# Inverse norms ahead of ELU work on ScalarE, and ELU's maximum moved between ScalarE and VectorE in three steps

## The chip, the cores and the metric

The kernel runs on one core of one Trainium2 chip. The metric is the device time of one execution in microseconds (us), as the median of several executions. The profile of one execution shows a span that is about 1.8 us shorter than that execution's device time, because the time also holds what lies outside the first and last instruction.

## The reference, cut to what matters

A linear attention feeds a two-layer perceptron:

```python
# q, k, v: (8, 8, 576, 64); g_norm: (64,); w_in: (512, 2048); w_out: (2048, 512)
kv = np.einsum('bhsd,bhse->bhde', k, v)
out = np.einsum('bhsd,bhde->bhse', q, kv)
rms = np.sqrt(np.mean(out * out, axis=-1, keepdims=True) + 1e-06)
attn = out / rms * g_norm
x = attn.transpose(0, 2, 1, 3).reshape(8 * 576, 512)
h = x @ w_in
g = np.where(h > 0.0, h, np.exp(np.minimum(h, 0.0)) - 1.0)      # ELU
return g @ w_out
```

The 4608 rows of `x` are worked in nine groups (0 to 8) of 512.

## The kernel before

For each group, TensorE does the first product `mm1` in eight steps (`h_ps`, two PSUM banks a step, 8 matmuls), then the second product `mm2` (`o_ps`). Between them stands ELU: ScalarE takes the exponential from PSUM, and VectorE does `min(e, 1) - 1` and then the maximum with `h`. The maximum reads `h` from PSUM, so it is what frees the two banks. With `relu`, ScalarE copies `relu(h)` out of PSUM first, so ScalarE frees the banks, and VectorE adds from SBUF instead.

```python
def elu(T, i, ps, relu):
    ...
    for lo, hi, h in parts:
        nc.scalar.activation(e[:, lo:hi, :], h, AF.Exp)
    if relu:
        r = mlpt.tile([P, 2, G], BF16, name="elu_h", tag="elu_h", bufs=2)
        for lo, hi, h in parts:
            nc.scalar.activation(r[:, lo:hi, :], h, AF.Relu)
        parts = [(0, 2, r)]

    def rest():
        nc.vector.tensor_scalar(out=e, in0=e, scalar1=1.0, scalar2=1.0, op0=ALU.min, op1=ALU.subtract)
        for lo, hi, h in parts:
            nc.vector.tensor_tensor(
                out=gT[T][:, 2 * i + lo : 2 * i + hi, :], in0=e[:, lo:hi, :], in1=h,
                op=ALU.add if relu else ALU.max)
    return rest
```

While a group's `mm1` runs, the attention of the next group is worked in pieces, for each half `h` of its rows: `se` (TensorE's score product into the PSUM tile `at`, of which there is one, and the square on ScalarE), `sum` (VectorE), `inv` (ScalarE: Ln, then Exp of -0.5 times that), `mul` (VectorE scales `at` into `xs`, which frees `at`, and the DMA engines transpose `xs` into `xT`), and `gain` (VectorE multiplies `xT` by `g_norm`). Group 1 is written out by hand, group 2 uses `window`:

```python
at = attention(2)
rest = {}
for i, tag in enumerate("mBAmBAmB"):        # PSUM banks: m (two single ones), pair A, pair B
    rest[i] = mm1(1, i, tag, i in (4, 5, 7))    # the last argument: relu
    if i == 2: at["kv"]()
    if i == 3: at["se0"]()
    if i == 5:
        at["sum0"](); at["inv0"](); at["mul0"](); rest[4]()
    if i == 6:
        at["se1"](); rest[5]()
    if i < 4: rest[i]()
at["sum1"](); at["inv1"](); rest[6](); at["mul1"](); rest[7]()
...                                         # then group 1's second product, its first tiles in pair A
def window(T, at, early, late, second):
    for i in range(8):
        rest = mm1(T, i, "BA"[i % 2])           # no relu
        for name in early.get(i, ()): at[name]()
        if i in second: second[i]()             # a piece of the second product of group T - 1
        rest()
        for name in late.get(i, ()): at[name]()
# T == 2:
early = {2: ("sum0", "inv0"), 5: ("sum1", "inv1"), 6: ("gain0",), 7: ("gain1",)}
late = {0: ("kv",), 1: ("se0",), 2: ("mul0",), 4: ("se1",), 5: ("mul1", "ahead")}
```

(Some lines are joined here, and "..." marks cuts.) In the traces each engine works through its own instructions in the order in which they are written: in the profile below, a Ln whose input was complete at 59.40 us starts at 61.62, behind two relus and an exponential (58.91 to 61.76) that stand ahead of it in the program.

## Time and profile before

The median is 291.17 us, of 3 executions between 291.03 and 291.43.

The profile's page gives the busy share of each engine and the granted TensorE clock in 40 slices of the span (tenths; 9 is 90% or more):

```profile
PE 276.6 (96%) x2085; PEld 128.8 (45%) x2121; DVE 167.4 (58%) x225; ACT 138.1 (48%) x201; POOL 49.2 (17%) x89
...
PEclk9999999999999999999999999999999999999999
```

TensorE (PE) is busy for 96% of the span at full clock. So the other engines cost time only where TensorE waits for them. The view of waits, for TensorE between 46 and 103 us (engine, its line and what it waited for: us in total, times, longest):

```profile
PE at L250 <- DVE xs L299: 2.1, 1, 2.1
PE h_ps L378 <- DVE xT L312: 0.9, 2, 0.4
PE h_ps L378 <- DVE gT L362: 0.4, 2, 0.2
```

The longest is explained by the timeline (start in us, length in us, engine, line, what is written from what, count; in brackets the idle time before it and what ended it):

```profile
56.05 5.35 PE L378 MATMUL h_ps<-xT,w_in_sb 128*128 128x512 bf16 x24
...
58.18 1.22 DVE L283 TENSOR_REDUCE ss<-sq 128x16 f32<-128x1024 bf16 x1
58.91 1.02 ACT L354 ACTIVATE elu_h<-h_ps 128x1024 bf16<-128x1024 f32 x1
59.81 1.03 ACT L350 ACTIVATE elu_e<-h_ps 128x1024 bf16<-128x1024 f32 x1
60.72 1.04 ACT L354 ACTIVATE elu_h<-h_ps 128x1024 bf16<-128x1024 f32 x1
...
61.62 0.33 ACT L291 ACTIVATE ss<-ss,eps_col 128x16 f32<-128x16 f32 x1
61.98 0.22 ACT L292 ACTIVATE ss<-ss 128x16 f32<-128x16 f32 x1
...
62.23 1.23 DVE L299 TENSOR_TENSOR xs<-at,ss 128x1024 bf16<-128x1024 f32 x1 [2.83 <-ACT ss L292]
...
63.50 0.41 PE L250 MATMUL at<-kv_sb,qT 64*128 64x64 bf16 x16 [2.10 <-DVE xs L299]
...
69.16 1.22 DVE L299 TENSOR_TENSOR xs<-at,ss 128x1024 bf16<-128x1024 f32 x1
...
74.23 0.49 DVE L312 TENSOR_SCALAR xT<-xT,g_col 128x1024 bf16<-128x1024 bf16 x1 [2.39 <-DMA xT<-xs]
...
74.82 1.89 PE L378 MATMUL h_ps<-xT,w_in_sb 128*128 128x512 bf16 x7 [0.44 <-DVE xT L312]
```

VectorE's sums (`ss<-sq`) are complete at 59.40. But the Ln and Exp of those sums stand in ScalarE's queue behind a relu, an exponential and another relu, and end at 62.20. Only then can VectorE scale `at` into `xs` (62.23 to 63.46), and only then can TensorE write its next scores into `at`, at 63.50. TensorE's last 24 matmuls before that start at 56.05. Counted with one 512-column matmul each 0.216 us (the eight from 63.85 to 65.58 us in this profile take 1.73 us), the slot of the last one (the time until the next could start) ends at 61.24. So TensorE stands idle for 2.26 us. The view of waits says 2.10, because it counts from the modelled end of the matmul, 61.40.

The second scale (69.16) leads, over the transposes, to the gain that ends at 74.72, and TensorE starts group 2 at 74.82.

### The profile page before, as it was taken

The page shows a single profiled execution, that of the slowest core. Times are in us where ns is not written, and L with a number is a line of the kernel's source. Part 1 is how long each engine was busy: PE and PEld are TensorE (multiplying, and loading weights), DVE is VectorE, ACT ScalarE, POOL GpSimd, SP SyncE. Part 2 cuts the span into 40 slices and gives each one's busy share as a digit, 9 for nine tenths or more (in the row PEclk, how much of TensorE's full clock was granted, in tenths as well). Part 3 has the DMA queues.
Part 4 walks back from the last instruction along what each step waited for, and adds up shares of the span by engine and source line. Part 5 has one row for each costly group of instructions (what it writes and reads, how often), then busy time and mean ns, then how long its engine had stood idle before and what let it go on. Part 6 is the DMA issues. An engine that isn't in the chain of part 4 may idle for free.

```text
span 288.4 us, 5107 instructions
## 1 busy us (share of the span) xinstructions
PE 276.6 (96%) x2085; PEld 128.8 (45%) x2121; DVE 167.4 (58%) x225; ACT 138.1 (48%) x201; POOL 49.2 (17%) x89
## 2 busy tenths in 40 slices
PE   7899999979999999999999999999999999999994
PEld 3444444434444344444444444444444444444443
DVE  3349732869278647862786377637774776344600
ACT  3578358683365345534554355425552555343311
POOL 7643303323034033003300330000000000000000
PEclk9999999999999999999999999999999999999999
DMA  7999999899799669869935892542140235030222
GB/s 210 184 204 206 206 270 220 182 278 137 119 259 166 136 105 286 107 116 253 222 41 102 227 239 66 93 101 73 36 97 15 73 39 109 0 75 0 73 73 74
DMA packets 50571, 39.46 MB, mean 137 GB/s; under 512 B 30964, under 2 KB 44020, under 8 KB 50548
## 3 DMA queue, kind: packets, MB, share of 16 engines
q0 software_dynamic: 15008, 21.30, 37.0%
q1 hardware_dynamic: 35136, 17.31, 30.4%
q10 hardware_dynamic: 404, 0.53, 0.5%
q8 instruction: 16, 0.26, 0.4%
q14 instruction: 7, 0.06, 0.1%
HBM read 36.70 MB, written 9.44 MB: 160 GB/s over the span
## 4 chain that ended last, share of the span: by engine, by line
PE 85%; DVE 6%; DMA 4%; issue 2%; ACT 2%; SPq 1%; DVEq 0%
PE h_ps L378 38%; PE o_ps L399 37%; DVE gT L362 2%; PE h_ps L566 2%; DMA first_v<-in_v_dram 2%; DMA xT<-xs 2%; PE at L250 2%; PE at L156 1%; PE o_ps L436 1%; DVE elu_e L358 1%; PE kv_ps L156 1%; DVE xs L299 1%; PE mean L199 1%; DVE ss L283 1%; ACT elu_e L350 1%
## 5 line engine op out<-in xcount | busy, mean ns | idle before, releaser
L399 PE MATMUL o_ps<-w_out_sb,gT 128*128 128x512 bf16 x548 | 128.6, 379 | 0.7 <-issue 0.2
L378 PE MATMUL h_ps<-xT,w_in_sb 128*128 128x512 bf16 x530 | 126.5, 379 | 2.3 <-DVE xT L312 0.9
L350 ACT ACTIVATE elu_e<-h_ps 128x1024 bf16<-128x1024 f32 (+1 forms) x79 | 74.1, 954 | 92.1 <-PE h_ps L378 81.2
L362 DVE TENSOR_TENSOR gT<-elu_e,h_ps 128x1024 bf16<-128x1024 bf16 (+1 forms) x73 | 81.1, 1118 | 7.2 <-PE h_ps L378 0.5
L399 PEld LDWEIGHTS <-gT 128*128 128x128 bf16 x560 | 54.4, 98 | 65.8 <-issue 0.9
L378 PEld LDWEIGHTS <-w_in_sb 128*128 128x128 bf16 x552 | 52.3, 98 | 63.2 <-DVE xT L312 0.9
L358 DVE TENSOR_SCALAR elu_e<-elu_e 128x1024 bf16<-128x1024 bf16 x72 | 32.3, 449 | 64.8 <-ACT elu_e L350 64.8
L415 ACT COPY o_sb<-o_ps 128x512 f32<-128x512 f32 x32 | 18.4, 588 | 23.8 <-PE o_ps L399 23.1
L103 POOL CAST q_bf<-st_q 128x384 bf16<-128x384 f32 x36 | 18.1, 546 | 34.3 <-DMA st_q<-in_q_dram 34.3
L283 DVE TENSOR_REDUCE ss<-sq 128x16 f32<-128x1024 bf16 x14 | 17.0, 1218 | 4.9 <-ACT sq L277 4.9
L299 DVE TENSOR_TENSOR xs<-at,ss 128x1024 bf16<-128x1024 f32 x14 | 17.1, 1219 | 2.8 <-ACT ss L292 2.8
L277 ACT ACTIVATE sq<-at 128x1024 bf16<-128x1024 f32 x14 | 14.4, 1026 | 0.8 <-PE at L250 0.8
L339 POOL COPY gate<-qT 1x32 bf16<-1x32 bf16 x5 | 1.0, 199 | 69.1 <-DMA qT<-q_bf 69.1
L212 DVE SCALAR_TENSOR_TENSOR xT<-y_ps,g_col,rT 128x512 bf16<-128x512 f32 (+1 forms) x10 | 6.2, 641 | 11.0 <-ACT rT L209 9.0
L312 DVE TENSOR_SCALAR xT<-xT,g_col 128x1024 bf16<-128x1024 bf16 x14 | 6.7, 481 | 4.5 <-DMA xT<-xs 4.5
L156 PEld LDWEIGHTS <-k_bf 64*64 64x64 bf16 x576 | 6.3, 107 | 5.6 <-issue 5.6
L90 POOL DMA_DIRECT2D k_bf<-in_k_dram x11 | 7.9, 722 | 2.6 <-DMA w_in_sb<-in_moe_w_in_dram 1.8
L90 POOL DMA_DIRECT2D v_bf<-in_v_dram x11 | 7.7, 697 | 4.2 <-DMA w_in_sb<-in_moe_w_in_dram 2.1
L250 PE MATMUL at<-kv_sb,qT 64*128 64x64 bf16 (+1 forms) x248 | 6.1, 192 | 2.1 <-DVE xs L299 2.1
L250 PEld LDWEIGHTS <-qT 64*128 64x128 bf16 (+1 forms) x248 | 4.4, 97 | 8.2 <-issue 8.0
L112 DVE COPY o_sb<-o_ps 128x256 f32<-128x256 f32 x1 | 0.4, 425 | 11.1 <-PE o_ps L436 11.1
L354 ACT ACTIVATE elu_h<-h_ps 128x1024 bf16<-128x1024 f32 x6 | 6.2, 1030 | 0.0
(55 smaller groups left out, 100.8 us busy)
## 6 DMA issues: line engine op xcount, KB each, us to landing
st_q<-in_q_dram POOLq DMA_DIRECT2D x6, 1152.0 KB, 7.0
out_dram<-o_sb SPq DMA_DIRECT2D x24, 256.0 KB, 3.3
k_bf<-in_k_dram POOLq DMA_DIRECT2D x6, 576.0 KB, 9.2
v_bf<-in_v_dram POOLq DMA_DIRECT2D x6, 576.0 KB, 12.3
out_dram<-o_sb SPq DMA_DIRECT2D x19, 128.0 KB, 2.4
w_out_sb<-in_moe_w_out_dram POOLq DMA_DIRECT2D x4, 512.0 KB, 15.0
w_in_sb<-in_moe_w_in_dram POOLq DMA_DIRECT2D x2, 512.0 KB, 11.0
q_bf<-in_q_dram POOLq DMA_DIRECT2D x3, 288.0 KB, 13.4
```

Source lines behind the costliest of these rows:

```text
L90: eng.dma_start(out=dst.rearrange("p m j d -> p m (j d)"), in_=in_[:, ms, :])
L103: nc.gpsimd.tensor_copy(out=bf["q", b][:, u, js], in_=raw[b][:, u::2, js, :].rearrange("p l j d -> p j l d"),)
L250: nc.tensor.matmul(se_ps[lo:hi, l, (4 * i + m) * 64 : (4 * i + m) * 64 + 64], lhsT=qT[b][l * 64 : l * 64 + 64, s, u, j : j + n, :], rhs=kv ...
L277: nc.scalar.activation(sq, st["se", h], AF.Square)
L283: nc.vector.reduce_sum(out=ss, in_=st.pop(("sq", h)).rearrange("p l (m e) -> p (l m) e", e=D), axis=AX.X,)
L299: nc.vector.tensor_tensor(out=st["xs"][:, 2 * h : 2 * h + 2, :].rearrange("p i (l m e) -> p l i m e", l=2, e=D), in0=se_ps.rearrange("p l ...
L350: nc.scalar.activation(e[:, lo:hi, :], h, AF.Exp)
L358: nc.vector.tensor_scalar(out=e, in0=e, scalar1=1.0, scalar2=1.0, op0=ALU.min, op1=ALU.subtract)
L362: nc.vector.tensor_tensor(out=gT[T][:, 2 * i + lo : 2 * i + hi, :], in0=e[:, lo:hi, :], in1=h, op=ALU.add if relu else ALU.max,)
L378: nc.tensor.matmul((ps[a] if isinstance(ps, list) else ps[:, a, :])[:, cols], lhsT=w_in_sb[:, c, f * P : f * P + P], rhs=xT[T][:, c, cols] ...
L399: nc.tensor.matmul(o_ps[T, j], lhsT=gT[T][:, f, j * P : j * P + P], rhs=w_out_sb[:, f, :], start=(f == 0), stop=(f == FC - 1),)
L415: nc.scalar.copy(o_sb[T, half][:, j % 2, :], o_ps[T, j])
```

## The change

The intent is to compute the inverse norms as soon as their sums are there, and to balance ELU's maximum: in group 1's step 5 it goes from ScalarE back to VectorE, and in group 2's steps 3 and 5 from VectorE to ScalarE. The second scale of group 1 (`mul1`) is also written ahead of step 6's work on VectorE. `"later"` returns the relu as a function of its own, so that the inverse norms can be written ahead of it.

```diff
-        if relu:
+        def freed():
             r = mlpt.tile([P, 2, G], BF16, name="elu_h", tag="elu_h", bufs=2)
             for lo, hi, h in parts:
                 nc.scalar.activation(r[:, lo:hi, :], h, AF.Relu)
-            parts = [(0, 2, r)]
+            parts[:] = [(0, 2, r)]
+        if relu and relu != "later":
+            freed()
 ...
-        return rest
+        return (freed, rest) if relu == "later" else rest
 ...
-        rest[i] = mm1(1, i, tag, i in (4, 5, 7))
+        rest[i] = mm1(1, i, tag, "later" if i in (4, 7) else False)
+        if i < 4:
+            rest[i]()
         if i == 2:
             at["kv"]()
         if i == 3:
             at["se0"]()
-        if i == 5:
+        if i == 4:
             at["sum0"]()
             at["inv0"]()
+            freed, rest[4] = rest[4]
+            freed()
+        if i == 5:
             at["mul0"]()
             rest[4]()
+            rest[5]()
         if i == 6:
             at["se1"]()
-            rest[5]()
-        if i < 4:
-            rest[i]()
     at["sum1"]()
     at["inv1"]()
+    at["mul1"]()
+    freed, rest[7] = rest[7]
+    freed()
     rest[6]()
-    at["mul1"]()
     rest[7]()
 ...
-    def window(T, at, early, late, second):
+    def window(T, at, early, late, second, relu=()):
         for i in range(8):
-            rest = mm1(T, i, "BA"[i % 2])
+            rest = mm1(T, i, "BA"[i % 2], i in relu)
 ...
-        window(T, at, early, late, second)
+        window(T, at, early, late, second, (3, 5) if T == 2 else ())
```

## The prediction

> **What bounds it.** TensorE: 276.6 of 288.4 us busy (96%) in the engine table, full clock in every slice, 85% of the chain of waits. VectorE (58%) and ScalarE (48%) matter only where TensorE waits for them. The change touches 48 to 100 us of the timeline. A 512-column matmul starts every 0.216 us; stepped with that, TensorE's gaps there are:
>
> - 61.45 to 63.50: group 2's second score product waits 2.05 us for `xs` (VectorE) to free `at`.
> - 74.2 to 74.82: 0.6 us for group 2's gained `xT`.
> - 88.80 to 88.97 and 94.15 to 94.51: 0.5 us for the maximum that frees pair A in group 2's steps 3 and 5.
> - 99.7 to 100.27: 0.6 us for group 3's gained `xT`.
>
> So at most 3.75 us is to be had.
>
> **Group 1.** The 2.05 us is ScalarE's queue: the sums end at 59.40, but Ln and Exp (0.33 + 0.22 us) stand behind relu 4, exp 5 and relu 5 (1.02 us each) and end at 62.20. Afterwards they follow exp 4 and end near 60.0; `xs` is done near 61.3, before TensorE asks. All 2.05 us goes.
>
> Given back: without step 5's relu, pair A is freed by a VectorE maximum instead of ScalarE (61.76). VectorE runs scale (1.22), step 4 (0.57 + 0.7) and step 5 (0.43 + 1.22) from 60.05: free near 64.3. TensorE wants A near 63.55: a new wait of about 0.75 us. The maximum takes 1.22 us, the add from SBUF 0.69[...].
>
> The second scale ends near 67.3 instead of 70.4. [...] transposes took 6.5 us to land while loads ran (to 68 us), later ones 2.4. So part of those 3 us is lost; I estimate `xT` gained at 72 to 72.5. TensorE finishes its 40 matmuls (8.85 us from 64.35) at 73.2, without a wait. Group 2 starts there instead of at 74.82: **1.6 us saved**.
>
> **Group 2.** Two more 1.02 us ScalarE activations find room (12.8 us busy of 25). They free A about 1.5 us sooner and shorten a VectorE operation from 1.22 to 0.69. The A waits go, but TensorE then waits longer for `xT`; only what the second scale gains counts. Ln starts as before, since the sums end only then. **About 0.4 us saved.**
>
> ScalarE gets one activation more in all.
>
> **Prediction:** 291.17 - 2.0 = 289.2 us, 8 in 10 between 288.4 and 290.2. Faster by over 2%: 0.02; within 2%: 0.97; slower by over 2%: 0.01.
>
> **What would show it.** The TensorE wait for `xs` is gone; Ln of the first norms starts near 59.5; a new TensorE wait for the `gT` maximum, 0.5 to 1 us, precedes group 1's second product, which ends without a wait for `xT`; group 2's waits for `gT` are gone, and one for `xT` remains near its end, as long or longer.
>
> **What would make it wrong.** GpSimd's casts (from 63.2 us) may slow VectorE (its min/subtract took 0.57 and 0.72 us there, not 0.43), so that A comes later. The second transposes may land later behind the loads. In group 2, stores or loads may delay the last transposes (4.1 us from scale to landing) or, begun earlier, let them land sooner.

Its sum is 1.6 + 0.4 = 2.0 us; the operation times, 1.22 and 0.69 us, and the landing times, 6.5 and 2.4 us, are read from the trace.

## More of the kernel before

With each execution comes the mean clock that TensorE was granted, as a share of full speed.

The profiled execution took 290.18 us.

## The result, and the profile after

The changed kernel took 288.5 us in the median, the kernel before 291.1 in the same rounds. The ratio is 0.9905, with a 95% interval of 0.9886 to 0.9925. A ratio here is the mean time of one kernel's fast runs over that of the other's of the same rounds, so it is not quite the ratio of the medians. The saving was 2.6 to 2.8 us where I had said 2.0. The median lies 0.1 us inside my range, and 0.9905 of 291.1 us is 288.3, just below it.

One of the four executions, the profiled one, took 484.63 us at a mean clock of 0.559, and is slow. Its profile says nothing about the change and is not used. I ran the changed kernel again under the label `again`. Its profiled execution took 288.27 us, and what follows is read from it. Line numbers have moved: the maximum or add that writes `gT` was L362 and is L366, min/subtract was L358 and is L362.

The waits of TensorE between 46 and 103 us, changed kernel:

```profile
PE h_ps L382 <- DVE xT L312: 0.9, 1, 0.9
PE o_ps L403 <- DVE gT L366: 0.5, 1, 0.5
```

The timeline of the changed kernel, for the same stretch as above:

```profile
58.47 1.21 DVE L283 TENSOR_REDUCE ss<-sq 128x16 f32<-128x1024 bf16 x1
59.72 0.31 ACT L291 ACTIVATE ss<-ss,eps_col 128x16 f32<-128x16 f32 x1 [0.63 <-DVE ss L283]
60.06 0.22 ACT L292 ACTIVATE ss<-ss 128x16 f32<-128x16 f32 x1
60.18 1.00 ACT L355 ACTIVATE elu_h<-h_ps 128x1024 bf16<-128x1024 f32 x1
60.31 1.23 DVE L299 TENSOR_TENSOR xs<-at,ss 128x1024 bf16<-128x1024 f32 x1 [0.62 <-ACT ss L292]
...
61.59 0.41 PE L250 MATMUL at<-kv_sb,qT 64*128 64x64 bf16 x16
...
63.10 1.22 DVE L366 TENSOR_TENSOR gT<-elu_e,h_ps 128x1024 bf16<-128x1024 bf16 x1
...
64.38 8.79 PE L403 MATMUL o_ps<-w_out_sb,gT 128*128 128x512 bf16 x40 [0.55 <-DVE gT L366]
...
66.08 1.22 DVE L299 TENSOR_TENSOR xs<-at,ss 128x1024 bf16<-128x1024 f32 x1 [0.62 <-ACT ss L292]
...
71.26 0.49 DVE L312 TENSOR_SCALAR xT<-xT,g_col 128x1024 bf16<-128x1024 bf16 x1 [0.42 <-DMA xT<-xs]
...
73.01 1.89 PE L382 MATMUL h_ps<-xT,w_in_sb 128*128 128x512 bf16 x7
```

The wait of 2.1 us for `xs` is gone. Ln starts at 59.72, `xs` is written by 61.54, and TensorE's scores start at 61.59. The slot of the last matmul before them ends at 61.33, so 0.26 us of the gap are left here, and 0.10 us in a second profile of the same kernel (`again_b`, below). In its place stands the new wait that I expected: pair A is now freed by VectorE's maximum (63.10 to 64.32), and TensorE starts the second product at 64.38, 0.72 us after the slot of its last matmul ended (61.93 + 8 x 0.216 = 63.66). The second scale now starts at 66.08 instead of 69.16, its `xT` is gained by 71.75, and group 2 starts at 73.01, without a wait for it.

The profile of the changed kernel spans 286.5 us, that of the kernel before 288.4. That is 1.9 us, almost exactly my 2.0. So the puzzle is not in these two profiles. It is why the timed executions differ by 0.7 us more than the profiled ones.

### The profile page after: what moved, and what is told of

Read it like the earlier page. It is cut to its first block, busy times and chain, and to the rows that moved or that the text cites. A ratio compares the mean times of both kernels' runs of the same rounds, so it can differ in the third digit from the quotient of the medians.

```text
span 482.8 us, 5110 instructions
## 1 busy us (share of the span) xinstructions
PE 470.4 (97%) x2085; PEld 170.3 (35%) x2121; DVE 166.4 (34%) x225; ACT 140.4 (29%) x202; POOL 47.8 (10%) x89
## 4 chain that ended last, share of the span: by engine, by line
PE 97%; issue 2%; DVE 0%; DVEq 0%
PE o_ps L403 44%; PE h_ps L382 43%; PE h_ps L570 2%; PE o_ps L440 1%; PE at L250 1%; PE at L156 1%; PE kv_ps L526 1%; PE qt_ps L174 1%; PE kv_ps L156 1%; PE mean L199 1%; PE mean L526 0%; PE y_ps L189 0%; PE y_ps L526 0%; DVE kv_sb L112 0%; DVE o_sb L112 0%
## 5 line engine op out<-in xcount | busy, mean ns | idle before, releaser
L403 PE MATMUL o_ps<-w_out_sb,gT 128*128 128x512 bf16 x548 | 222.7, 582 | 2.2 <-issue 1.2
L382 PE MATMUL h_ps<-xT,w_in_sb 128*128 128x512 bf16 x530 | 215.5, 579 | 3.9 <-issue 2.4
L403 PEld LDWEIGHTS <-gT 128*128 128x128 bf16 x560 | 72.7, 131 | 139.6 <-issue 137.8
L382 PEld LDWEIGHTS <-w_in_sb 128*128 128x128 bf16 x552 | 70.6, 131 | 128.5 <-issue 125.6
L362 DVE TENSOR_SCALAR elu_e<-elu_e 128x1024 bf16<-128x1024 bf16 x72 | 30.7, 427 | 216.3 <-ACT elu_e L350 216.3
L366 DVE TENSOR_TENSOR gT<-elu_e,h_ps 128x1024 bf16<-128x1024 bf16 (+1 forms) x72 | 79.8, 1116 | 7.4 <-DVE elu_e L362 0.9
L103 POOL CAST q_bf<-st_q 128x384 bf16<-128x384 f32 x36 | 16.8, 509 | 31.8 <-DMA st_q<-in_q_dram 27.6
L156 PEld LDWEIGHTS <-k_bf 64*64 64x64 bf16 x576 | 7.9, 131 | 8.8 <-issue 8.0
L570 PE MATMUL h_ps<-xT,w_in_sb 128*128 128x512 bf16 x24 | 9.8, 579 | 0.0
L112 DVE COPY qT<-qt_ps 128x1024 bf16<-128x1024 bf16 (+1 forms) x8 | 3.3, 453 | 12.6 <-PE qt_ps L174 12.6
```

Source lines behind the costliest of these rows:

```text
L103: nc.gpsimd.tensor_copy(out=bf["q", b][:, u, js], in_=raw[b][:, u::2, js, :].rearrange("p l j d -> p j l d"),)
L156: nc.tensor.matmul(kv_ps[s][l * 64 : l * 64 + 64, u * 64 : u * 64 + 64], lhsT=bf["k", b][rows, 2 * l + u, j, :], rhs=bf["v", b][rows, 2 * ...
L366: nc.vector.tensor_tensor(out=gT[T][:, 2 * i + lo : 2 * i + hi, :], in0=e[:, lo:hi, :], in1=h, op=ALU.add if relu else ALU.max,)
L382: nc.tensor.matmul((ps[a] if isinstance(ps, list) else ps[:, a, :])[:, cols], lhsT=w_in_sb[:, c, f * P : f * P + P], rhs=xT[T][:, c, cols] ...
L403: nc.tensor.matmul(o_ps[T, j], lhsT=gT[T][:, f, j * P : j * P + P], rhs=w_out_sb[:, f, :], start=(f == 0), stop=(f == FC - 1),)
L570: nc.tensor.matmul(h[a] if isinstance(h, list) else h[:, a, :], lhsT=w_in_sb[:, c, (2 * i + a) * P : (2 * i + a) * P + P], rhs=xT[0][:, c, :],
```

## The experiments

Twelve runs were made, in three sets of four; those of one set ran on one chip, with the kernel before beside them. All gave correct results.

### The changed kernel again, its two halves, and one variant

`again` is the changed kernel, unedited. `g1` keeps only the part in group 1, and `g2` only the part in group 2:

```diff
 g1, against the changed kernel:
-        window(T, at, early, late, second, (3, 5) if T == 2 else ())
+        window(T, at, early, late, second, ())
 g2, against the kernel before:
-            rest = mm1(T, i, "BA"[i % 2])
+            rest = mm1(T, i, "BA"[i % 2], i in relu)
-        window(T, at, early, late, second)
+        window(T, at, early, late, second, (3, 5) if T == 2 else ())
 keep5, against the changed kernel:
-        rest[i] = mm1(1, i, tag, "later" if i in (4, 7) else False)
+        rest[i] = mm1(1, i, tag, "later" if i in (4, 7) else i == 5)
```

> The changed kernel itself, because its profile fell in a slow state (granted clock 0.559). Theory 1 (my sums were right in kind): start of group 2's first product moves from 74.8 to about 73.2 us, the wait for pair A is 0.5 to 1 us, and the extra gain over my 2.0 us sits in group 2 (transposes landing sooner). Theory 2: the wait for pair A is shorter than 0.75 us, so that group 2 starts near 72.5, and group 2 saves the 0.4 us that I put down. Time near 288.4 us, ratio 0.990 to 0.992.

> Only the part of the change in group 1; group 2 keeps its maximum on VectorE in every step. Theory 1 (group 1 saves 1.6 us as predicted): 289.5 us, ratio 0.9945. Theory 2 (the extra gain is in group 1): 288.8 us or less, ratio 0.992 or lower.

> Only the part of the change in group 2: the kernel before, with relu on ScalarE in steps 3 and 5. Theory 1 (the extra gain is here): about 290.0 us, ratio 0.9965. Theory 2 (0.4 us as predicted): 290.7 us, ratio 0.9985. If the two parts only work together, their savings will not add up to the whole of about 2.7 us.

> The changed kernel with relu kept on ScalarE in group 1's step 5, so that ScalarE again frees pair A. If the wait for pair A is a loss that ends in the time, as predicted, this is up to 0.7 us faster than the change (about 287.8 us), with pair A free near 62.9 instead of 64.3 us. If the later transposes set the start of group 2, the saved wait turns into a wait for xT and the time stays at about 288.4 us.

| kernel | median, us | ratio to before | 95% interval |
|---|---|---|---|
| before, same rounds (11 executions) | 290.72 | | |
| again | 288.49 | 0.9941 | 0.9914 to 0.9967 |
| g1 | 288.12 | 0.9913 | 0.9892 to 0.9934 |
| g2 | 291.54 | 1.0020 | 0.9996 to 1.0045 |
| keep5 | 288.31 | 0.9933 | 0.9908 to 0.9958 |

Neither theory of `again` held: the wait for pair A was 0.72 us, and group 2 did not give the extra gain. The second theory of `g1` held: group 1's part gives all of the gain that the times show, and group 2's part none of it. `g2` is no faster than the kernel before, and `g1` is no slower than the whole change. `keep5` removed the wait for pair A as expected (group 2 then started at 72.68), but group 3 started at 98.33 against 98.36 in `again`, and its time is that of the change. I return to that below.

The larger finding was in the list of executions. The kernel before was now at 290.72, not 291.17, and its 11 executions fell into two heaps: seven between 289.81 and 290.90 us at a mean clock of 0.999 or 1.000, and four between 291.05 and 291.51 us, all at 0.994. The same was true of `g2`: four of six executions at 0.994, at 291.48 us and more, and two at 0.999. No execution of `again`, `g1` or `keep5` was at 0.994.

The profiled execution of `g2` happened to be one of those at 0.994. In group 1 it is the kernel before, so it shows what happens there. This is the table of windows of `g2` (window in us; its length and the busy time and count of each engine; then the granted clock, the DMA share, and GB/s):

```profile
64.00:64.50 0.50, 0.50 (x12) 0.19 (x5) 0.47 (x2) 0.32 (x1) 0.50 (x2) 0.65 1.20 207
...
65.00:66.00 1.00, 1.00 (x3) 0.34 (x3) 0.97 (x2) 0.21 (x1) 1.00 (x3) 0.50 1.22 209
...
67.50:68.00 0.50, 0.50 (x4) 0.25 (x3) 0.43 (x2) 0.32 (x1) 0.00 (x0) 0.94 1.28 225
68.00:70.00 2.00, 2.00 (x11) 0.92 (x10) 1.29 (x2) 1.97 (x4) 0.00 (x0) 1.00 0.52 95
```

The clock is granted in full up to 64.15 us (0.65 is the mean of a window that is 30% at 1.00 and 70% at 0.50), is one half until 67.56 us, and is full again after that. That is 3.41 us at half speed, right behind TensorE's gap, which in this execution lasts from 61.48 to 63.74 us, 2.26 us again. In the stretch at half speed, group 1's last eight first-product matmuls took from 64.08 to 67.44 us, 3.36 us instead of 1.73:

```profile
63.74 0.41 PE L250 MATMUL at<-kv_sb,qT 64*128 64x64 bf16 x16 [2.10 <-DVE xs L299]
...
67.44 8.86 PE L399 MATMUL o_ps<-w_out_sb,gT 128*128 128x512 bf16 x40
```

The page of the profile of the kernel before shows full clock in every slice only because that one execution was of the other kind.

That gave a new theory: the gap that the change removes costs more than its own length, because in about half of the executions the clock drops behind it. The rival: the drops come at random, or belong to the chip's state.

### Filling the gap without moving anything

If the gap itself is the cause, then filling it with useless matmuls in the kernel before must end the drops, although no useful work comes sooner.

```diff
 fill, against the kernel before (fill5: 5 in place of 9):
         if i == 6:
+            idle(9, pair("B", "idle_ps")[:, 0, :])     # matmuls of zeros, result thrown away
             at["se1"]()
```

Pair B is free at that time, since group 1's relu of step 4 has read it.

> The kernel before, with nine matmuls of zeros (about 1.94 us) put into TensorE's 2.05 us gap of group 1; their result is thrown away, nothing else moves. Theory A (the gap itself lets the granted clock drop to half for some 3.4 us in part of the executions of the kernel before, which show a mean clock of 0.994 and 1.2 us more time): no execution of this kernel shows 0.994, its times lie near 290.2 us, about 0.3% below the mean of the kernel before. Theory B (the drops come at random or belong to the chip's state): a share of executions near that of the kernel before, 4 of 11, again shows 0.994 at about 291.4 us.

> The kernel before with only five matmuls of zeros in the 2.05 us gap, which leaves some 1.0 us idle. If the gap causes the clock drops, and only a long one does, no execution shows 0.994 (as with nine matmuls), and times are near 290.2 to 290.5 us. If any gap of 1 us suffices, or if the drops are random, about half of the executions show 0.994 and 291.3 us, as in the kernel before (11 of 22 so far).

The timelines of TensorE, first `fill`, then `fill5`:

```profile
61.42 2.11 PE L522 MATMUL idle_ps<-zeros 128*128 128x512 bf16 x9
63.68 0.41 PE L250 MATMUL at<-kv_sb,qT 64*128 64x64 bf16 x16 [0.16 <-DVE xs L299]
```

```profile
61.74 1.24 PE L522 MATMUL idle_ps<-zeros 128*128 128x512 bf16 x5
64.01 0.41 PE L250 MATMUL at<-kv_sb,qT 64*128 64x64 bf16 x16 [1.02 <-DVE xs L299]
```

| kernel | median, us | executions at clock 0.994 | ratio to before | 95% interval |
|---|---|---|---|---|
| fill (0.3 us of idle time left) | 290.53 | 0 of 6 | 0.9982 | 0.9958 to 1.0005 |
| fill5 (1.2 us of idle time left) | 290.49 | 0 of 6 | 0.9988 | 0.9953 to 1.0023 |
| before, all three sets | | 16 of 33 | | |

The idle times left are counted from the end of the last matmul's slot; the profile's waits, from the modelled end of the matmul, are 0.16 and 1.02 us. The drops are gone in both. If each execution still dropped with the share of 16 in 33, none in 12 would happen about once in 3000 times, so chance is ruled out, and so is the chip's state: the kernel before dropped beside both, on the same chips and in the same rounds (7 of 11, and 5 of 11). That the gap causes the drops is shown. The times alone would not have shown it: the ratios' intervals include 1, and the filled kernels' mean of 290.4 us lies 0.2 us above that of the executions of the kernel before without a drop. I have not looked for that 0.2 us.

What the profiles show of the drop is little. In `g2` the gap of 2.26 us was followed by 3.41 us at half clock. In the profiled execution of the kernel before, a gap of the same length (61.24 to 63.50 us) was not: its table of windows gives a clock of 1.00 from 63.5 to 75 us. In the profile of `g1` TensorE stood idle for 1.57 us ahead of group 2, and the table of windows gives a clock of 1.00 around it and after it (70 to 75 and 75 to 90 us). Only one profiled execution, that of `g2`, has the mean clock of 0.994, so the length of 3.41 us rests on one profile. Why the same gap is followed by a drop in 16 of 33 executions and not in the others is not shown, nor is the length from which a gap has this effect.

### Why group 2's part gained nothing

In the changed kernel TensorE's two waits for pair A in group 2 are gone, and still group 2 is not shorter. From its key-value product to that of group 3 TensorE takes 27.19 us in the kernel before, 27.09 in `again`. I had expected 0.4 us from the second scale being sooner. Lines of the timeline, kernel before:

```profile
93.23 1.22 DVE L362 TENSOR_TENSOR gT<-elu_e,h_ps 128x1024 bf16<-128x1024 bf16 x1
...
93.89 1.29 SPq L457 DMA_DIRECT2D out_dram<-o_sb  x2
...
94.37 1.22 DVE L299 TENSOR_TENSOR xs<-at,ss 128x1024 bf16<-128x1024 f32 x1
...
95.62 2.83 SPq L306 DMA_TRANSPOSE xT<-xs  x2
...
99.73 0.49 DVE L312 TENSOR_SCALAR xT<-xT,g_col 128x1024 bf16<-128x1024 bf16 x1 [2.08 <-DMA xT<-xs]
...
100.27 1.04 PE L378 MATMUL h_ps<-xT,w_in_sb 128*128 128x512 bf16 x4 [0.43 <-DVE xT L312]
```

and the changed kernel (`again`):

```profile
91.11 0.69 DVE L366 TENSOR_TENSOR gT<-elu_e,elu_h 128x1024 bf16<-128x1024 bf16 x1
...
91.72 1.22 DVE L299 TENSOR_TENSOR xs<-at,ss 128x1024 bf16<-128x1024 f32 x1
91.79 1.29 SPq L461 DMA_DIRECT2D out_dram<-o_sb  x2
...
93.17 3.38 SPq L306 DMA_TRANSPOSE xT<-xs  x2
...
97.81 0.49 DVE L312 TENSOR_SCALAR xT<-xT,g_col 128x1024 bf16<-128x1024 bf16 x1 [2.65 <-DMA xT<-xs]
...
98.36 0.82 PE L382 MATMUL h_ps<-xT,w_in_sb 128*128 128x512 bf16 x3 [0.85 <-DVE xT L312]
```

VectorE's last ELU operation ahead of the scale is shorter, 0.69 instead of 1.22 us, and the scale does come sooner: it starts 0.07 us ahead of the two stores of 256 KB (`out_dram<-o_sb`) instead of 0.48 behind. But the stores still stand ahead of the transposes in the SP queue. The `xT` they give starts to be gained 5.8 us after the stores' issue before, and 6.0 us after it in the change. Counted from the end of the scale, it takes 4.1 us before and 4.9 us after. So TensorE waits for `xT` longer than it did, 0.85 us in the view of waits of the change against 0.43. Most of the delay shows in the SP queue, which took 3.38 us to issue the two transposes behind the stores instead of 2.83. `keep5` starts group 2 sooner by 0.3 us and loses that to the same wait (1.20 us).

Theory: the transposes wait for the stores, in the queue or on the DMA engines. Rival: their landing is set by something else. The test issues those stores after the transposes:

```diff
 defer, against the changed kernel (keep5_defer: against keep5; g1_defer: against g1):
-        if j % 2 == 1:
+        if j % 2 == 1 and (T, half) != (1, 1):
             store(T, half)
 ...
-            late = {0: ("kv",), 1: ("se0",), 2: ("mul0",), 4: ("se1",), 5: ("mul1", "ahead")}
+            late = {0: ("kv",), 1: ("se0",), 2: ("mul0",), 4: ("se1",), 5: ("mul1", "store", "ahead")}
+            at["store"] = lambda: store(1, 1)
```

> The group 1 part alone once more, for a profile of its usual time: most of its runs took 287.9 to 288.4 us, the profiled one 289.7. Theory: in the usual execution group 2 starts near 73.1 us as in the changed kernel, and the 0.3 us by which this kernel was below the changed kernel comes in group 2: its stores and the last transposes meet less, and group 3 starts near 98.1 us. Rival: the 0.3 us was noise between runs, and this time both are equal at 288.4.

> The changed kernel with group 1's last two stores of 256 KB issued after group 2's last two score transposes instead of before them. Theory (in the changed kernel the sooner scale of step 5 gains nothing, because the transposes stand behind those stores): the transposes land about 3.8 us after the scale instead of 4.9, the TensorE wait for xT ahead of group 3 shrinks from 0.85 us to nearly nothing, and the time falls by 0.8 to 1.0 us, to about 287.5. Rival (the landing is set by something else, such as the order of the transposes themselves): no change, 288.4.

> The same late stores, and relu kept on ScalarE in group 1's step 5, which started group 2 at 72.7 us instead of 73.0 but gained nothing in the time, as group 3 waited for xT until 98.3 us all the same. If the stores were what took it back, this is the fastest kernel: 287.1 to 287.3 us, 0.3 us below the one with late stores alone. If not, both are equal.

The timeline of `defer`, for the same stretch:

```profile
91.78 1.22 DVE L299 TENSOR_TENSOR xs<-at,ss 128x1024 bf16<-128x1024 f32 x1
...
93.03 2.50 SPq L306 DMA_TRANSPOSE xT<-xs  x2
...
95.62 1.29 SPq L461 DMA_DIRECT2D out_dram<-o_sb  x2
96.83 0.49 DVE L312 TENSOR_SCALAR xT<-xT,g_col 128x1024 bf16<-128x1024 bf16 x1 [1.60 <-DMA xT<-xs]
...
97.40 1.89 PE L382 MATMUL h_ps<-xT,w_in_sb 128*128 128x512 bf16 x8
```

The gain now starts 3.83 us after the scale's end instead of 4.87, and group 3 starts at 97.40 instead of 98.36 us. TensorE shows no wait for `xT` there. From group 2's to group 3's key-value product it takes 26.05 us, 1.04 less than in `again`. The theory holds: the stores ahead of the transposes took back what the sooner scale gained. Issuing the transposes took 2.50 us here. The timelines say where the time was lost: the SP queue was done issuing both transposes at 96.55 us in `again` and at 95.53 in `defer`, and the gain starts 1.26 and 1.30 us after that. So it was lost before the end of the issue, in the SP queue.

The time fell less than the 0.8 to 1.0 us that I expected: the median of `defer` was 288.02 us (ratio 0.9903, 0.988 to 0.9927), that of `keep5_defer` 288.06 (0.9899, 0.9871 to 0.9928). `keep5_defer` is thus no faster than `defer`, and these intervals overlap those of the changed kernel, so that the profiles show the gain in group 2, but the times do not show one. Both profiles show a new wait in group 3. These are its lines in `keep5_defer`:

```profile
119.32 0.49 DVE L312 TENSOR_SCALAR xT<-xT,g_col 128x1024 bf16<-128x1024 bf16 x1 [1.24 <-DMA xT<-xs]
...
120.25 1.22 DVE L366 TENSOR_TENSOR gT<-elu_e,h_ps 128x1024 bf16<-128x1024 bf16 x1
...
121.52 0.81 PE L382 MATMUL h_ps<-xT,w_in_sb 128*128 128x512 bf16 x3 [0.52 <-DVE gT L366]
```

VectorE stood idle for 1.24 us until transposes landed, in order to do the first gain (119.32), which nothing needs yet. Behind it in VectorE's queue stood the ELU step whose maximum frees TensorE's banks, and TensorE waited 0.52 us for that.

`g1_b` is `g1` once more. It gave 288.19 us (0.9917, 0.989 to 0.9944), and its profile, of an execution of 287.92 us, has group 2 started at 72.77 and group 3 at 97.98 us. Group 2 is then 26.95 us long, against 27.09 in `again`. So group 2's part of the change is worth nothing while the stores are in the way. Whether it costs the 0.4 us between the medians of `g1` and `again` in the first set is not settled, since the intervals overlap widely. The later medians, 288.19 of `g1_b` and 288.23 of `again_b` on another chip, do not repeat it.

### Late stores without relu in group 2, the combination, and the change once more

> The group 1 part with the late stores, without relu in group 2. Theory (relu in group 2 gains only once the stores are out of the way): TensorE's waits for pair A in group 2 (0.2 and 0.35 us) are back, and the stretch from group 2's to group 3's key-value product is 26.4 to 26.6 us, 0.4 to 0.5 more than the 26.05 with relu and late stores. Rival (relu in group 2 is worth nothing or harmful in itself): 26.1 us or less.

> Relu kept in group 1's step 5, late stores, and group 3's first gain one step later on VectorE (its wait for a landing held the maximum behind it and cost TensorE 0.5 us at 121.5 us in the kernel with the first two). If that wait was all that took back the late stores' gain, group 3 runs 29.3 us long again instead of 30.0, and the usual time is 286.6 to 286.9 us, the fastest kernel. If the DMA traffic moves the wait elsewhere, it stays at 287.1 to 287.3 us.

> The changed kernel once more, on the same chip as the other three, for comparison and a second usual profile: 288.3 to 288.5 us in most runs, no execution at 0.994, group 2 to group 3 27.1 us.

`g1_defer` took 26.53 us in group 2, within the 26.4 to 26.6 that the theory gave, and 0.48 more than `defer`. So the relu in group 2 is worth about 0.5 us, but only once the stores are out of the way. Of the two waits for pair A that the theory named, only the first is back (0.17 us in the view of waits). The rest is an `xT` that came later: group 3 starts at 99.65, 0.29 us after the slot of the last matmul before it. That profile is of an execution that started group 2 late, so the number rests on one profile of an unusual execution. As a kernel its median is higher than that of `g1` (289.0 us; 0.9949, 0.9913 to 0.9985; the intervals overlap): in group 3 of its profile TensorE waited 1.0 us for the maximum behind the gain.

`best` is `keep5_defer` with one line more:

```diff
+        if T == 3:
+            early = {2: ("sum0", "inv0"), 4: ("sum1", "inv1"), 6: ("gain0",), 7: ("gain1",)}
```

Its median is 287.12 us, ratio 0.9891 (0.9853 to 0.9929). The stretch from group 3's to group 4's key-value product is 29.33 us, as in `again`, where `keep5_defer` took 30.01. The view of waits lists none of TensorE between 46 and 135 us in its profile. So the profile shows what the theory named, while the median is what the rival named (287.1 to 287.3), with two of the six executions at 288.7 and 288.8 us. It is the lowest median of all, 1.1 us below that of the change on the same chip (`again_b`: 288.23 us; 0.9918, 0.9886 to 0.995), but the intervals overlap, so that `best` is faster than the change is not shown by the times.

`again_b` confirms the rest: no execution at 0.994, a span of 286.4 us, 27.16 us from group 2 to group 3.

## Why the prediction was right or wrong

Over all sets, by the clock of each execution (fast runs only; for the changed kernel these are the three of the first result, `again` and `again_b`):

| | executions | median, us | mean, us |
|---|---|---|---|
| before, clock 0.998 to 1.000 | 17 | 290.10 | 290.16 |
| before, clock 0.994 | 16 | 291.28 | 291.34 |
| changed, clock 0.998 to 1.000 | 15 | 288.42 | 288.55 |

At equal clock, the change saves 290.10 - 288.42 = 1.7 us in the median. A drop costs 291.34 - 290.16 = 1.2 us. In the rounds of the first result the four executions of the kernel before took 291.00 to 291.43 us. Their clocks were not listed, but by their times they belong to the second row, so there the saving was about 1.7 + 1.2 = 2.9, against 2.6 to 2.8 measured. With the mix of all sets (means 290.73 and 288.55) it is 2.2 us.

Point by point:

- **TensorE bounds the kernel, and the whole gap of 2.05 us goes: right but for the size.** The gap was 2.26 us, and 0.26 us (`again`) or 0.10 us (`again_b`) are left of it. Ln starts at 59.72 (I said near 59.5), the wait for `xs` is gone.
- **The new wait for pair A: right.** I said about 0.75 us with A free near 64.3; it was 0.72, with the maximum ending at 64.32. Two errors cancel in it: the scale started at 60.31 and not 60.05, and step 4's min/subtract took 0.42 us and not 0.57.
- **The second scale ends near 67.3, `xT` gained at 72 to 72.5, no wait for it: right**, or on the safe side: 67.30 and 71.75.
- **Group 1 saves 1.6 us: slightly low.** Group 2 started at 73.01 instead of 74.82, 1.8 us sooner; by its key-value product (76.64 before) `again` and `again_b` are 1.8 and 2.0 us sooner. I had given the 40 matmuls 8.85 us, to 73.2; they took 8.63 (64.38 to 73.01).
- **Group 2 saves 0.4 us: wrong.** It went from 27.19 to 27.09 and 27.16 us. The step that failed is "only what the second scale gains counts". The scale was sooner against the stores by 0.55 us, but its transposes were issued behind the stores in the queue, and TensorE's wait for `xT` grew from 0.43 to 0.85 us. I had named stores as a risk and still put the gain into the sum. Issuing them later brought 1.04 us in group 2. That my 1.6 + 0.4 came so near the 1.9 us of the profiles is in part luck: the one was too low and the other too high.
- **"full clock in every slice": right for the profiled execution, wrong for the kernel.** The sum has no term for what a gap does to the clock. 16 of 33 executions of the kernel before had a mean clock of 0.994, at a cost of 1.2 us each. The 0.006 that they lack are 1.7 us of 289, which is what 3.41 us at half clock, as in the profile of `g2`, take away. The change ends that: of 56 fast executions of the kernels that hold its group 1 part, none was at 0.994.
- **"291.17 - 2.0": wrong, and with the missing clock term this is the step that failed and moved the result to the edge of my range.** I read the saving from an execution of 290.18 us, and subtracted it from a median of executions that had lost about 1 us more. From 290.18 the same 2.0 us gives 288.2, and the changed kernel's executions have a median of 288.42. What the runs show in place of 2.0 us is 1.7 us at equal clock, and 1.2 us more against an execution with a drop.
- **"within 2%": right.**

Three things stay open. One is the exact condition for a drop. Another is why a few executions at full clock take 0.6 to 2 us more (288.98, 289.11 and 290.43 of the changed kernel's 15): in the profiles of `g1` and `g1_defer`, executions of this kind at 289.71 and 290.67 us, TensorE waited 1.4 and 1.5 us for `xT` ahead of group 2. In `g1` the loads beside these transposes were late too: between 70 and 76 us the queue of GpSimd's loads (q0) still moved 8 packets, where `again`, `keep5` and `g2` show none. What held up the loads is not known. The third is the 0.2 us of the filled kernels.

## What to carry to other kernels

A gap of TensorE can cost more than its length, because the clock may drop behind it, in some executions and not in others (here 1.2 us more behind a gap of 2.26 us, in 16 of 33). So compare the profiled execution's time and clock with those of the timed ones before subtracting a saving from a median, and look at each execution's clock before comparing two kernels to half a per cent. A scale on VectorE that came sooner by 0.55 us against the stores gained nothing here while its transposes stood in the SP queue behind two stores of 256 KB that nobody waits for (the gain began 4.9 us after the scale's end, and 3.8 us with the stores behind the transposes), so the saving has to be followed to the instruction that TensorE waits for.
